# Three chained stages on one core: 128 queries an attention step from rearranged inputs, one ring for all weights, and a written order for the last stage

## The chip, the core and the metric

The kernel runs on one core of a Trainium2 chip. A core has five engines with an instruction queue each: TensorE (PE; its weight loads are listed apart as PEld), VectorE (DVE), ScalarE (ACT), GpSimd (POOL) and SyncE (SP, which here only issues DMAs). Data is brought from HBM by 16 DMA engines into SBUF, a memory of 128 partitions; TensorE writes its products into PSUM, eight banks of 2 KB a partition. The metric is the device time of one execution in microseconds (us), taken as the median of several runs.

## The reference

Everything is chained: the attention's output is the input of the mixture of experts, whose output is the input of the last network.

```python
# 1 attention: B,H,S,D = 2,8,768,64; a query sees keys nearer than 16 and 24 block summaries
k_sum = k.reshape(B, H, 24, 32, D).max(axis=3)
v_sum = v.reshape(B, H, 24, 32, D).mean(axis=3)
scores_l = where(abs(pos_q - pos_k) < 16, scale * q @ k.T, -1e9)
scores_s = scale * q @ k_sum.T + log(32)
a = softmax(concat([scores_l, scores_s]))      # sum + 1e-9 below
x = a @ concat([v, v_sum])                     # -> 1536 tokens x 512
# 2 experts: E = 8, w1[e] 512x1024, w2[e] 1024x512
do = x @ w_skip > 0
e = argmax(x[do] @ w_gate);  gate = softmax(x[do] @ w_gate)[e]
x[do] += gate * relu(x[do] @ w1[e]) @ w2[e]
# 3 last network: w_in 512x2048, w_out 2048x512, alpha 2048 (w_in and w_out in float64)
h = x @ w_in
out = (max(h, 0) + alpha * min(h, 0)) @ w_out
```

## The kernel before

**Attention.** A step takes 64 queries of all 8 heads; there are 24 steps. q and k arrive as they lie in memory, and TensorE transposes them (lines 187, 240 and 268). The transposed queries are put into a tile `qbd` in which the two heads of a pair stand on the diagonal with zeros beside them, so that one matmul with 128 rows and 128 columns gives both heads. A step is: a matmul that writes the mask (`s<-mask,sel`, L284), four score matmuls (L286), the maximum on DVE (`nm`, L289), four exponentials on ACT that also sum (`p`, L293), a product with the reciprocal sum on POOL (L305), four transposes (`pt`, L311) and their copy (`ts`, L315), eight matmuls with the values (`xp`, L327; a query sees a window of 96 keys and 24 summaries, so 120 rows). After each 128 tokens the result is transposed (`xtp`, L420), multiplied with the gate weights (`lt`, L432) and folded into the routing logits (`lg`, L442). The block means of v come for the first batch from a matmul with an averaging matrix (`vps`, L231), for the second from POOL. Everything here stands in a written order.

**Experts.** 64 tokens an expert are computed always, in pairs of experts that share one gather (`xg`); `rest` computes further tokens behind a branch where an expert has more than 64. TensorE and ACT follow the written order; DVE and POOL are ordered by a scheduler. `gpa` (L892) is the transposition of gathered tokens, `ph` (L945) the first product, `hT` (L904) the transposed hidden values, `py` (L965) the second product, `hx` (L981) the last pair's result, which `x2q` (L1108) adds to the tokens.

**Last network.** 48 units (n, j): n is one of three blocks of 512 tokens, j one of 16 slices of 128 hidden columns. A unit is 12 matmuls up (`g`, L1219) and, two units later, 12 matmuls down (`o`, L1242). Each factor is a sum of a high and a low part, and three of the four products are formed. w_in and w_out come as float64 and are turned into float32 on DVE and ACT in chunks (`f`, L641 to L649: one chunk is 128 x 512 in three steps, which the code asks for with `fill`), and split by ACT into the high part (L1182) and by POOL into the low part (`wl`, L1183). PReLU is `gs` (L1222 and L1223), its parts `ghi` (L1225, ACT) and `glo` (L1227, POOL). `prep_x2` transposes the next tokens (`x2p`, L1204) and splits them (`xl`, L1081). In this stage the scheduler orders all engines.

`F2` says after which expert how many steps of conversion are asked for. Six chunks are asked for there; the split of the first weights stands in the last network's loop:

```python
F2 = (0, 0, 3, 3, 3, 3, 3, 3)
    if c == 0 and n == 0:
        split_in(j)
        fill(FJ)          # FJ = 5
        split_out(j)
    up(n, j)
    if c == 0 and j == 1 and n + 1 < NBL:
        prep_x2(n + 1)
```

Of the kernel before, what the change touches and what calls it, by code (L numbers as in the profile page):

```python
# [22 lines left out]

def bf16_parts(x, n):
    out = []
    for _ in range(n):
        b = (np.float32(x).view(np.uint32) + np.uint32(0x8000)) & np.uint32(0xFFFF0000)
        h = float(b.view(np.float32))
        out.append(h)
        x = x - h  # L30
    return out


@with_exitstack
def tile_kernel(ctx: ExitStack, tc: tile.TileContext, q, k, v, w_skip, w_gate, w1, w2, w_in, w_out, alpha, out):
    nc = tc.nc
    B, H, S, D = q.shape
    NP = H // 2
    NS = S // 64
    NB = S // 32  # L40
    NC = S // 256
    NK = 120
    LT = 3
    LX = 4
    NV = 4
    RB = 4
# [11 lines left out]
    HE = E // 2  # L58

    const = ctx.enter_context(tc.tile_pool(name="const", bufs=1))  # L60
    ring = ctx.enter_context(tc.tile_pool(name="ring", bufs=8))
# [13 lines left out]
    qbd = []  # L75
    for i in range(2):
        qbd.append(apool.tile([128, 4, NP, 2, 64], F32, name=f"qbd{i}"))

    def clear(t, eng):
        eng.memset(t[0:64, :, :, 1, :], 0.0)  # L80
        eng.memset(t[64:128, :, :, 0, :], 0.0)

    clear(qbd[0], nc.vector)


    sel = apool.tile([67, 128], BF16, name="sel")
    nc.gpsimd.memset(sel, 1.0)
    nc.gpsimd.memset(sel[0:64, :], 0.0)
    nc.gpsimd.affine_select(
        out=sel[0:64, :].rearrange("p (h x) -> p h x", h=2), in_=sel[0:64, :].rearrange("p (h x) -> p h x", h=2),  # L90
        pattern=[[0, 2], [-1, 64]], compare_op=ALU.not_equal, fill=1.0, base=0, channel_multiplier=1,
    )
    mask = apool.tile([67, 3, NK], BF16, name="mask")
    nc.gpsimd.memset(mask, 0.0)
    logs = bf16_parts(math.log(32.0), 3)
    mlog = mask[64:67, :, 96:NK]
    nc.gpsimd.memset(mlog, logs[0])
    for i in (1, 2):
# [26 lines left out]
    def win(s):
        return (0, 0) if s == 0 else ((2, 32) if s == NS - 1 else (1, 16))

    vt = [apool.tile([NK, NV, H * D], F32, name=f"vt{b}") for b in range(B)]
    xs = {}

    kst, qst, kw, vbk, st = {}, {}, {}, {}, {}
    late, after = [], []
    V, A, P = nc.vector.tensor_copy, nc.scalar.copy, nc.gpsimd.tensor_copy
    ka, kb, km, spare = {}, {}, {}, []

    def load(src, b, c, tag):
        pool, rt_, n = (kpool, "raw", RB) if tag != "qst" else (apool, "qraw", 1)
        raw = pool.tile([128, H, 2, D], F32, tag=rt_, bufs=n, name=f"raw{tag}{b}_{c}")
        nc.sync.dma_start(raw, src[b, :, 256 * c:256 * c + 256, :].rearrange("h (p r) d -> p h (r d)", r=2))
        st[tag, b, c] = raw  # L140

    def stage(b, c, tag, bufs, eng):
        t = (kpool if tag == "kst" else apool).tile([128, 2, H, D], F32, tag=tag, bufs=bufs, name=f"{tag}{b}_{c}")
        eng(t.rearrange("p r h d -> p h r d"), st.pop((tag, b, c)))
        (kst if tag == "kst" else qst)[b, c] = t

    vbd = dram.tile([B, H, NB, D], F32, name="vbd")

    def load_vblk(b, i):
        src = v[b, 4 * i:4 * i + 4].rearrange("h (n t) d -> (h n) (t d)", t=32)  # L150
        for u in range(2):
            t = kpool.tile([96, 16, D], F32, tag="raw", bufs=RB, name=f"vbk{b}_{i}_{u}")
            nc.sync.dma_start(t, src[:, 16 * D * u:16 * D * u + 16 * D])
            vbk[b, i, u] = t

    def mean_v(b, i, step):
        t, t1 = vbk[b, i, 0], vbk[b, i, 1]
        if step < 2:
            w = slice(8 * step, 8 * step + 8)
            nc.gpsimd.tensor_tensor(out=t[:, w, :], in0=t[:, w, :], in1=t1[:, w, :], op=ALU.add)  # L160
        elif step == 2:
            nc.gpsimd.tensor_tensor(out=t[:, 0:8, :], in0=t[:, 0:8, :], in1=t[:, 8:16, :], op=ALU.add)
        else:
            for w in (4, 2, 1):
                nc.gpsimd.tensor_tensor(out=t[:, 0:w, :], in0=t[:, 0:w, :], in1=t[:, w:2 * w, :], op=ALU.add)
            m = kpool.tile([96, D], F32, tag="vm", bufs=2, name=f"vm{b}_{i}")
            nc.gpsimd.tensor_scalar(out=m, in0=t[:, 0, :], scalar1=1.0 / 32.0, scalar2=None, op0=ALU.mult)
            st["vm", b, i] = m

    def put_v(b):  # L170
        for i in range(2):
            nc.sync.dma_start(vbd[b, 4 * i:4 * i + 4].rearrange("h n d -> (h n) d"), st["vm", b, i])
        for j in range(NV):
            nc.sync.dma_start(
                vt[b][96:NK, j, :].rearrange("n (h d) -> n h d", h=H), vbd[b].rearrange("h n d -> n h d"))

    def load_vwin(b, s):
        k0 = 64 * s - win(s)[1]
        nc.sync.dma_start(
            vt[b][0:96, s % NV, :].rearrange("p (h d) -> p h d", h=H),  # L180
            v[b, :, k0:k0 + 96, :].rearrange("h p d -> p h d"),
        )

    def first_k(c):
        def part(ps, n, dst, src):
            x = kst[0, src][:, r, 2 * g:2 * g + 2, :].rearrange("p h d -> p (h d)")
            nc.tensor.transpose(ps[:, r, dst:dst + n], x[128 - n:128], ident[128 - n:128, 128 - n:128])

        if c == 0:
            for g in range(NP):  # L190
                (pool, tag) = ((ps_s, "s"), (ps_s, "s"), (ps_t, "t"), (ps_t, "t"))[g]
                ka[g] = pool.tile([128, 2, 256], F32, tag=tag, name=f"ka{g}")
                kw[0, g] = kpool.tile([128, NS, NK], F32, tag="kw", bufs=NP, name=f"kw0_{g}")
                km[g] = apool.tile([128, NB], F32, tag="ks", bufs=4, name=f"ks0_{g}")
        if c == 1:
            for g in range(NP):
                (pool, tag) = ((ps_m, "m"), (ps_m, "m"), (ps_m, "m"), (ps_x, "x"))[g]
                full = pool.tile([128, 512], F32, tag=tag, name=f"kb{g}")
                kb[g] = full[:, 0:384].rearrange("p (r i) -> p r i", r=2)
                spare.append(full[:, 384:512])  # L200
        for g in range(NP):
            for r in range(2):
                part(*((ka[g], 128, 128 * c, c) if c < 2 else (kb[g], 128, 64, 2)))
        if c == 1:
            for g in range(NP):
                for r in range(2):
                    part(kb[g], 64, 0, 1)

    def first_max(half, g, eng=nc.vector):
        ps, o = (kb[g][:, :, 64:192], 16) if half else (ka[g], 0)  # L210
        n = ps.shape[2] // 16
        eng.tensor_reduce(
            out=km[g][:, o:o + n], in_=ps.rearrange("p r (n i) -> p n r i", n=n), axis=AX.XY, op=ALU.max)
# [1090 lines left out]
```

## Time and profile before

| what | us |
|---|---|
| runs | 544.91 to 545.46, median 545.08 |
| the profiled execution | 544.38 |
| its span, first to last instruction | 542.6 |
| PE, DVE, ACT, POOL busy in the span | 498.7, 313.4, 164.9, 193.9 |

The profiled execution is 1.8 us longer than the span, and 0.7 us below the median of the runs. A busy time is a sum over the whole span and says nothing about a stage; the rows below are therefore by stage. The granted clock is full speed where it reads 1.00. Each float32 matmul leaves two records in the trace, so that "x8" in a row is four matmuls.

### The profile page before, as it was taken

Reading aid. Unit: us, or ns where it says so; the run is one execution under the profiler, and the core shown is the slowest. Engines: PE = TensorE matmul, PEld = TensorE weight load, DVE = VectorE, ACT = ScalarE, POOL = GpSimd, SP = SyncE. Lnnn points to the kernel's source line nnn. Section 1 sums busy time; section 2 is a strip of 40 time slices with the busy share of each in tenths; the row PEclk is TensorE's granted clock in tenths of the full one; section 3 lists DMA queues with packets and bytes.
Section 4 is the critical chain, followed back from the end, with each engine's and each line's share of the span. In section 5 each row is a group of like instructions: output and inputs, shape, how many; then the busy total and the mean of one; then the engine's idle time right before and its main releaser. Section 6 shows DMA issues by size and latency. Waiting matters only on the chain.

```text
span 542.6 us, 8283 instructions
## 1 busy us (share of the span) xinstructions
PE 498.7 (92%) x2999; PEld 372.7 (69%) x2999; DVE 313.4 (58%) x632; ACT 164.9 (30%) x452; POOL 193.9 (36%) x196
## 2 busy tenths in 40 slices
PE   7988999978899999596499899999999999999997
PEld 5577888853454454265277788888888888888885
DVE  4579666476431854289999739893624324243333
ACT  3666677730011110333444442531120101101010
POOL 5285523336220310324853244733453221212121
PEclk9989999998999999898879999999999999999999
DMA  9899979863999583484445402210000000001022
GB/s 240 229 257 247 278 208 277 240 212 109 383 390 396 183 296 118 150 267 143 136 156 170 142 0 79 77 39 1 0 1 0 2 0 2 0 1 59 20 77 77
DMA packets 66820, 76.81 MB, mean 142 GB/s; under 512 B 23358, under 2 KB 46930, under 8 KB 66764
## 3 DMA queue, kind: packets, MB, share of 16 engines
q1 hardware_dynamic: 55916, 59.67, 35.4%
q10 hardware_dynamic: 9408, 14.68, 8.5%
q0 software_dynamic: 1440, 1.76, 1.0%
q8 instruction: 29, 0.48, 0.4%
q14 instruction: 27, 0.22, 0.1%
HBM read 71.00 MB, written 7.91 MB: 145 GB/s over the span
## 4 chain that ended last, share of the span: by engine, by line
PE 49%; DVE 4%; POOL 2%; issue 1%; DMA 1%; ACT 1%; ACTq 0%; POOLq 0%; DVEq 0%
PE o L1242 24%; PE g L1219 24%; POOL wl L1183 1%; DMA raw<-in_moe_w_in_dram 1%; PE ph L945 1%; DVE f L643 1%; DVE f L649 1%; DVE f L648 1%; DVE xl L1081 1%; DVE acc L1252 1%; PE x2p L1204 0%; DVE f L641 0%; POOL glo L1227 0%; ACT raw L644 0%; ACT acc L1250 0%
## 5 line engine op out<-in xcount | busy, mean ns | idle before, releaser
L1227 POOL TENSOR_TENSOR glo<-gs,ghi 128x512 fp32r<-128x512 f32 x48 | 66.7, 1390 | 157.1 <-ACT ghi L1225 157.1
L1222 DVE TENSOR_SCALAR gs<-g,al 128x512 f32<-128x512 f32 x48 | 35.9, 749 | 109.7 <-PE g L1219 109.7
L1225 ACT CAST ghi<-gs 128x512 fp32r<-128x512 f32 x48 | 29.9, 622 | 176.4 <-PE o L1242 150.9
L1242 PE MATMUL o<-woh,ghi 128*128 128x512 f32 x192 | 76.3, 397 | 5.3 <-ACT ghi L1225 5.3
L1242 PE MATMUL o<-woh,glo 128*128 128x512 f32 x192 | 76.4, 398 | 3.0 <-POOL glo L1227 3.0
L1242 PE MATMUL o<-wl,ghi 128*128 128x512 f32 x192 | 76.4, 398 | 0.0
L1219 PE MATMUL g<-xh,wih 128*128 128x512 f32 (+1 forms) x196 | 53.6, 395 | 2.7 <-DVE xl L1081 1.4
L1219 PE MATMUL g<-xl,wih 128*128 128x512 f32 (+1 forms) x196 | 53.0, 390 | 1.1 <-DVE xl L1081 1.1
L1219 PE MATMUL g<-xh,wl 128*128 128x512 f32 (+1 forms) x196 | 51.5, 385 | 0.0
L1242 PEld LDWEIGHTS o<-woh,ghi 128*128 128x128 f32 x192 | 36.4, 190 | 13.7 <-ACT ghi L1225 5.5
L1219 PEld LDWEIGHTS g<-xh,wih 128*128 128x128 f32 x196 | 36.8, 190 | 11.4 <-issue 1.7
L1242 PEld LDWEIGHTS o<-woh,glo 128*128 128x128 f32 x192 | 36.3, 189 | 11.9 <-POOL glo L1227 3.8
L1219 PEld LDWEIGHTS g<-xl,wih 128*128 128x128 f32 x196 | 36.6, 188 | 9.5 <-DVE xl L1081 1.5
L1242 PEld LDWEIGHTS o<-wl,ghi 128*128 128x128 f32 x192 | 36.5, 190 | 8.2
L1219 PEld LDWEIGHTS g<-xh,wl 128*128 128x128 f32 x196 | 36.4, 188 | 7.8
L945 PE MATMUL ph<-w,gTa 128*64 128x512 f32 x128 | 32.9, 626 | 9.4 <-PEq L1148 5.5
L305 POOL TENSOR_TENSOR p<-p,sm 128x480 f32<-128x480 f32 x23 | 24.1, 1049 | 47.2 <-DVE sm L304 21.5
L293 ACT ACTIVATE p<-s,nm 128x120 f32<-128x120 f32 x96 | 33.5, 365 | 22.7 <-DVE sm L303 19.7
L644 ACT ACTIVATE raw<-raw 128x512 f32<-128x512 f32 x32 | 21.7, 684 | 42.6 <-DVE f L643 41.0
L1223 DVE SCALAR_TENSOR_TENSOR gs<-g,gs 128x512 f32<-128x512 f32 x48 | 33.0, 687 | 1.0
L1183 POOL TENSOR_TENSOR wl<-f,wih 128x512 fp32r<-128x512 f32 x16 | 23.3, 1462 | 20.7 <-ACT wih L1182 18.7
L648 DVE SCALAR_TENSOR_TENSOR f<-raw,f 128x512 int32<-128x512 int32 x32 | 30.4, 954 | 0.3
(213 smaller groups left out, 816.4 us busy)
## 6 DMA issues: line engine op xcount, KB each, us to landing
w<-in_moe_w_dram SPq DMA_DIRECT2D x30, 1024.0 KB
raw<-in_moe_w_in_dram ACTq DMA_DIRECT2D x14, 512.0 KB
raw<-in_moe_w_out_dram ACTq DMA_DIRECT2D x14, 512.0 KB
vt<-in_v_dram SPq DMA_DIRECT2D x24, 192.0 KB
rawqst<-in_q_dram SPq DMA_DIRECT2D x6, 512.0 KB
rawkst<-in_k_dram SPq DMA_DIRECT2D x6, 512.0 KB
xd<-x SPq DMA_DIRECT2D x12, 256.0 KB
out_dram<-acc SPq DMA_DIRECT2D x12, 256.0 KB
```

Of the source, the lines that this page charges most:

```text
L293: nc.scalar.activation(p[:, g, :], sp[:, g, :], AF.Exp, bias=nm[:, g:g + 1], scale=1.0, accum_out=sm[:, g:g + 1])
L305: eng.tensor_tensor(out=p, in0=p, in1=sm.to_broadcast([128, NP, NK]), op=ALU.mult)
L644: nc.scalar.activation(raw.bitcast(F32)[:, :, 0], raw.bitcast(F32)[:, :, 1], AF.Abs)
L648: nc.vector.scalar_tensor_tensor(out=f, in0=m1, scalar=-0x40000000, in1=f, op0=ALU.bitwise_and, op1=ALU.bitwise_or)
L945: nc.tensor.matmul(hp[e][64 * h:64 * h + 64, :], gT[g][:, kc, o:o + 64], a[kc // 2][:, kc % 2, 512 * h:512 * h + 512], start=(kc == 0), st ...
L1183: nc.gpsimd.tensor_tensor(out=lo, in0=f, in1=hi.bitcast(F32), op=ALU.subtract)
L1219: nc.tensor.matmul(ph[:, o], a[:, kc, :], x[kc // 2][:, kc % 2, o], start=(i == 0), stop=(i == 3 * KC - 1))
L1222: nc.vector.tensor_scalar(out=g, in0=ph, scalar1=0.0, scalar2=al[:, j:j + 1], op0=ALU.min, op1=ALU.mult)
L1223: nc.vector.scalar_tensor_tensor(out=g, in0=ph, scalar=0.0, in1=g, op0=ALU.max, op1=ALU.add)
L1225: nc.scalar.copy(ghi, g)
L1227: nc.gpsimd.tensor_tensor(out=glo, in0=g, in1=ghi.bitcast(F32), op=ALU.subtract)
L1242: nc.tensor.matmul(po[i], a[:, o], x, start=(jj == 0 and p == 0), stop=(jj == JC - 1 and p == 2))
```

## The change

The host hands over q and k already transposed, v as windows with a column of ones behind each head, the gate and skip weights side by side and alpha as columns. A step of attention takes 128 queries, so there are 12. Scores are formed in 64 x 64 quarters of the array: r is the head of a pair (which rows of the array), c the half of the queries (which columns). The sum of a softmax comes out of the ones column, and the division is done on the 128 x 512 result by DVE (`sub_n`) instead of on the probabilities by POOL. All big tiles, from raw k to the split weights and the output's accumulators, share one ring of 17 places. In the expert stage DVE stands in a written order too; conversions begin one expert earlier (FC) and come to eight chunks; eight splits (EARLY) stand behind experts 5, 6 and 7. The last network is in a written order on all engines; its next tokens are prepared one or two tiles a unit.

```diff
-    ring = ctx.enter_context(tc.tile_pool(name="ring", bufs=8))
+    NRING = 17
+    ring = ctx.enter_context(tc.tile_pool(name="ring", bufs=NRING))
...
-    ps_m = att.enter_context(tc.tile_pool(name="ps_m", bufs=3, space=PSUM))
+    ps_m = att.enter_context(tc.tile_pool(name="ps_m", bufs=1, space=PSUM))
...
-        nc.tensor.matmul(sp, sel, mask[:, win(s)[0], None, :].to_broadcast([67, NP, NK]), start=True, stop=False)
-        for g in range(NP):
-            nc.tensor.matmul(
-                sp[:, g, :], d[:, s % 4, g].rearrange("p h x -> p (h x)"), kw[b, g][:, s, :], start=False, stop=(g == NP - 1))
...
+        for g in range(NP):
+            for c in range(2):
+                for r in range(2):
+                    o = 128 * (t % 2) + 64 * c
+                    nc.tensor.matmul(
+                        sp[r][64 * c:64 * c + 64, g, :], qs[64 * r:64 * r + 64, g, o:o + 64],
+                        kw[b, g][64 * r:64 * r + 64, 2 * t + c, :], start=False, stop=(g == NP - 1))
...
-            nc.scalar.activation(p[:, g, :], sp[:, g, :], AF.Exp, bias=nm[:, g:g + 1], scale=1.0, accum_out=sm[:, g:g + 1])
+            nc.scalar.activation(
+                p[:, g, :], st["s", n][r][:, g, :], AF.Exp, bias=st["nm", n][:, r, g:g + 1], scale=SCALE)
...
+        nc.vector.reciprocal(out=sm, in_=sm)
+        xs[n] = t = apool.tile([128, H * D], F32, tag="x", bufs=3, name=f"x{n}")
+        nc.vector.tensor_tensor(
+            out=t.rearrange("p (k h d) -> p k h d", k=2, h=4), in0=x[:, :, :, 0:D],
+            in1=sm.to_broadcast([128, 2, 4, D]), op=ALU.mult)
...
-    F2 = (0, 0, 3, 3, 3, 3, 3, 3)
+    FC = (0, 3, 3, 4, 4, 4, 4, 2)
...
-    me.enter_context(tc.manual_schedule(engines={mybir.EngineType.PE, mybir.EngineType.Activation}))
+    EARLY = {5: ((0, 0), (1, 0), (0, 1)), 6: ((1, 1), (0, 2), (1, 2)), 7: ((0, 3), (1, 3))}
+    me.enter_context(tc.manual_schedule(engines={mybir.EngineType.PE, mybir.EngineType.Activation, mybir.EngineType.DVE}))
...
+        for o, j in EARLY.get(n, ()):
+            (split_in, split_out)[o](j)
...
+    if MANUAL:
+        fe.enter_context(tc.manual_schedule())
+    for i, (n, j) in enumerate(work):
+        c, k = i // per, i % per
+        up(n, j)
+        if c == 0:
+            for t in {1: (4, 5), 2: (6, 7), 3: (8,), 4: (9,), 5: (10,), 6: (11,)}.get(k, ()):
+                prep_x2(t // NB2, t % NB2)
```

On PE, in the middle of the attention, one step of 64 queries before stands in these rows (`kw` are the key windows of a pair of heads, `qbd` the queries, `p` the probabilities):

```order
L284 LDWEIGHTS sel
L284 MATMUL s_11_1542<-mask,sel 128x480
L286 MATMUL s_11_1542<-kw_0_520,qbd_87 128x120
L286 MATMUL s_11_1542<-kw_1_585,qbd_87 128x120
L286 MATMUL s_11_1542<-kw_2_646,qbd_87 128x120
L286 MATMUL s_11_1542<-kw_3_766,qbd_87 128x120
L311 MATMUL pt_8_1559<-ident,p_8_1401 120x128 x4
L327 MATMUL xp_6_1518<-vt_132,ts_7_1538 64x64 x8
L432 MATMUL lt_1573<-xT_1540,wg 32x128 x4
```

One step of 128 queries of the changed kernel, of whose 16 score matmuls four and of whose eight groups of value matmuls two stand here (`s_0` and `s_1` are the banks of the two heads of a pair):

```order
L315 MATMUL lg_643<-fold,lts_600 128x9
...
L178 MATMUL s_0_646<-mask,sel 64x480
...
L178 MATMUL s_1_647<-mask,sel 64x480
...
L185 MATMUL s_0_646<-kw_0_128,q_2_161 64x120
L185 MATMUL s_1_647<-kw_0_128,q_2_161 64x120
...
L301 MATMUL xtp_668<-ident,x_627 128x128 x4
L207 MATMUL pt_0_684<-ident,p_0_576 120x128 x4
L207 MATMUL pt_1_691<-ident,p_1_602 120x128 x4
L309 MATMUL lt_698<-xT_673,wg 32x128 x4
L218 MATMUL xp_710<-vt_106,ts_0_586 64x65 x2
L218 MATMUL xp_710<-vt_106,ts_1_593 64x65 x2
```

A score matmul now fills 64 rows of its bank, and there are 16 where two steps before had eight; the logits of an earlier tile (`lg`) now open the step ahead of the scores, and `xtp` and `lt` of the next tile follow in the same step.

On DVE, at the passage from the experts to the last network, before (`f` are chunks under conversion, `hx` the last expert's result, `xl` the low parts of the tokens):

```order
L641 TENSOR_SCALAR f_5_4102<-raw_5_3969 128x512
L981 TENSOR_SCALAR hx_1972<-py_3864,lgate 64x256 x2
L649 SCALAR_TENSOR_TENSOR f_4_4020<-raw_4_3961,f_4_4020 128x512
L643 SCALAR_TENSOR_TENSOR f_5_4102<-raw_5_3969,f_5_4102 128x512
L641 TENSOR_SCALAR f_5_4152<-raw_5_4016 128x512
L1081 TENSOR_TENSOR xl_0_3894<-x2q_3827,xh_0_3892 128x2x128
L648 SCALAR_TENSOR_TENSOR f_5_4102<-raw_5_3969,f_5_4102 128x512
L1081 TENSOR_TENSOR xl_1_3895<-x2q_3827,xh_1_3893 128x2x128
L1081 TENSOR_TENSOR xl_0_3894<-x2q_3832,xh_0_3892 128x2x128
L649 SCALAR_TENSOR_TENSOR f_5_4102<-raw_5_3969,f_5_4102 128x512
```

The same passage of the changed kernel (`gs` is PReLU of the first units):

```order
L494 SCALAR_TENSOR_TENSOR f_3_3632<-raw_3_2954,f_3_3632 128x512
L774 TENSOR_SCALAR hx_1776<-py_3698,lgate 64x256 x2
L900 TENSOR_TENSOR xl_3723<-x2q_3657,xh_3722 128x2x128
L900 TENSOR_TENSOR xl_3723<-x2q_3662,xh_3722 128x2x128
...
L1014 TENSOR_SCALAR gs_0_3801<-g_0_3776,al 128x512
L1015 SCALAR_TENSOR_TENSOR gs_0_3801<-g_0_3776,gs_0_3801 128x512
L1014 TENSOR_SCALAR gs_1_3821<-g_1_3808,al 128x512
L1015 SCALAR_TENSOR_TENSOR gs_1_3821<-g_1_3808,gs_1_3821 128x512
L900 TENSOR_TENSOR xl_3829<-x2p_3832,xh_3828 128x2x128 x2
```

Between `hx` and the second `gs` no conversion is left on DVE; the conversions of j = 0 to 3 stand ahead of `hx`.

## Rows read from the trace of the kernel before

**Rows 1.** Stretches: us, busy PE, PEld, DVE, ACT, POOL, PEclk, DMA share, GB/s.
```profile
0.00:127.50 127.50, 114.34 (x1124) 92.26 (x1124) 84.28 (x272) 75.38 (x286) 56.30 (x95) 0.96 0.88 240
127.50:244.20 116.70, 104.85 (x648) 53.06 (x648) 56.97 (x113) 18.50 (x33) 27.69 (x25) 0.99 0.73 259
244.20:300.40 56.20, 41.37 (x197) 33.80 (x197) 54.30 (x82) 23.78 (x51) 29.94 (x19) 0.88 0.47 152
...
150.00:160.00 10.00, 9.69 (x78) 5.09 (x76) 4.14 (x10) 1.16 (x3) 2.87 (x3) 1.00 1.04 392
```
**Rows 2.** Chain of waits in the last network: start, us, engine, line.
```profile
306.13 2.76 PE g L1219 x12
311.66 2.76 PE g L1219 x12
...
530.22 6.27 PE o L1242 x27
```
**Rows 3.** Timeline of PE in the attention: start, us, line, form, records.
```profile
99.80 1.05 PE L286 MATMUL s<-kw,qbd 128*128 128x120 f32 x8
...
103.00 0.37 PE L284 MATMUL s<-mask,sel 67*128 67x480 bf16 x1
103.21 1.05 PE L286 MATMUL s<-kw,qbd 128*128 128x120 f32 x8
104.09 0.60 PE L311 MATMUL pt<-ident,p 128*120 128x128 f32 x4
104.62 1.15 PE L327 MATMUL xp<-vt,ts 120*64 120x64 f32 x16
105.70 0.42 PE L432 MATMUL lt<-xT,wg 128*32 128x128 f32 x8
106.55 0.66 PE L420 MATMUL xtp<-ident,x 128*128 128x128 f32 x4
107.22 0.39 PE L442 MATMUL lg<-fold,lts 128*128 128x9 f32 x2
```
**Rows 4.** The same view: block means of v.
```profile
17.79 5.33 PE L231 MATMUL vps<-rawvst,avg 128*24 128x512 f32 x12
```
**Rows 5.** Groups by line: busy, mean ns; idle before, releaser.
```profile
L289 DVE TENSOR_REDUCE nm<-s 128x4 f32<-128x480 f32 x24 | 15.7, 656 | 25.2 <-PE s L286 25.1
L293 ACT ACTIVATE p<-s,nm 128x120 f32<-128x120 f32 x96 | 33.5, 365 | 22.7 <-DVE sm L303 19.7
L293 ACT ACTIVATION_READ_ACCUMULATOR p<-s,nm 128x1 f32 x96 | 20.0, 208 | 0.0
L315 ACT COPY ts<-pt 120x512 f32<-120x512 f32 x24 | 14.2, 595 | 0.9 <-PE xp L327 0.9
...
L648 DVE SCALAR_TENSOR_TENSOR f<-raw,f 128x512 int32<-128x512 int32 x32 | 30.4, 954 | 0.3
...
L1222 DVE TENSOR_SCALAR gs<-g,al 128x512 f32<-128x512 f32 x48 | 35.9, 749 | 109.7 <-PE g L1219 109.7
```
**Rows 6.** Timeline of PE and DVE from the experts' start; waits in brackets.
```profile
127.50 0.66 PE L892 MATMUL gpa<-ident,xg 128*128 128x128 f32 x4 [0.80 <-DMA xg<-xd,lidx]
...
144.89 1.93 PE L945 MATMUL ph<-w,gTa 128*64 128x512 f32 x7 [1.47 <-issue]
...
226.57 3.26 PE L945 MATMUL ph<-w,gTa 128*64 128x512 f32 x8 [5.46 <-PEq L1148]
...
240.51 3.67 PE L965 MATMUL py<-w,hT 128*64 128x256 f32 x32 [0.56 <-DVE hT L904]
246.75 5.26 PE L1108 MATMUL x2q<-oc,hx 128*128 128x128 f32 x32 [2.57 <-DVE hx L981]
...
250.33 2.04 DVE L648 SCALAR_TENSOR_TENSOR f<-raw,f 128x512 int32<-128x512 int32 x1
...
267.03 0.80 PE L1242 MATMUL o<-woh,ghi 128*128 128x512 f32 x1 [5.26 <-ACT ghi L1225]
...
271.71 0.79 PE L1242 MATMUL o<-woh,glo 128*128 128x512 f32 x1 [3.04 <-POOL glo L1227]
```

More of the change, by code (lines that the diff above doesn't have):

```diff
@@ L21, with tile_kernel @@
 DRAM = bass.MemoryType.DRAM
[L24 to L31, printed above, removed]
 @with_exitstack
-def tile_kernel(ctx: ExitStack, tc: tile.TileContext, q, k, v, w_skip, w_gate, w1, w2, w_in, w_out, alpha, out):
+def tile_kernel(ctx: ExitStack, tc: tile.TileContext, qt, kt, vwin, vtok, vblk, wgs, als, w1, w2, w_in, w_out, out):
     nc = tc.nc
[L37 to L46, printed above, removed]
+    B, NCH, _, NP, QW = qt.shape
+    SP = kt.shape[3]
+    NTB, NWK, NV, H, DV = vwin.shape[1:]
+    D = DV - 1
+    S = NTB * 128
+    NB, NS = S // 32, S // 64
+    NK = NWK + NB
     SCALE = 1.0 / math.sqrt(D)
@@ L72, in tile_kernel @@
+    V, A, P = nc.vector.tensor_copy, nc.scalar.copy, nc.gpsimd.tensor_copy
+    xs, st, kw, qc, vt, vbk = {}, {}, {}, {}, [], {}
     ident = const.tile([128, 128], F32, name="ident")
     make_identity(nc, ident)
[L75 to L86, printed above, removed]
@@ L125, in win @@
[L125 to L140, printed above, removed]
@@ L142, in stage @@
[L142 to L154, printed above, removed]
@@ L201, in first_k @@
         for g in range(NP):
[L202 to L205, printed above, removed]
+            for c in range(2):
                 for r in range(2):
[L207 to L213, printed above, removed]
@@ new lines, in sub_t, with sub_x @@
+        copy(ts, pt)
+        st["ts", n, r] = ts
+    def sub_x(n):
+        b, t = divmod(n, NTB)
+        ts = [st.pop(("ts", n, r)) for r in range(2)]
+        st["x", n] = xp = ps_x.tile([128, 2, 512], F32, tag="x", name=f"xp{n}")
+        for h in range(H):
+            for c in range(2):
+                nc.tensor.matmul(
+                    xp[64 * c:64 * c + 64, h // 4, DV * (h % 4):DV * (h % 4) + DV],
+                    ts[h % 2][:, h // 2, 64 * c:64 * c + 64], vt[b][:, 2 * (t % 2) + c, h, :], start=True, stop=True)
@@ L678, in tile_kernel, with warm @@
+    def warm(n):
+        t = ps_t.tile([128, 512], F32, tag="t", name="warm")
+        for i in range(n):
+            nc.tensor.matmul(t, rt["ones"], rt["rows"].bitcast(BF16)[:, 0:512], start=True, stop=True)
     ms = ExitStack()
     ms.enter_context(tc.manual_schedule())
-    load(q, 0, 0, "qst")
-    for c in range(NC):
-        load(k, 0, c, "kst")
-    hot(HOT[0])
-    stage(0, 0, "qst", 1, V)
-    stage(0, 0, "kst", 3, V)
-    first_k(0)
-    prep_q(0, 0, 0, A)
-    prep_q(0, 0, 1)
-    for c in range(NC):
-        load(v, 0, c, "vst")
@@ L819, in tile_kernel @@
-    route_a(*G[2])
-    for t in range(4 + NPL, 8):
-        route_c(t)
-    sub_x(*subs[NN - 2])
-    tile_xt(TT - 2)
-    flush(late)
-    sub_x(*subs[NN - 1], copy=both)
-    tile_lt(TT - 2)
-    flush(late)
-    for f in todo[NN + 1]:
-        f()
-    tile_xt(TT - 1)
-    route_b(*G[2])
-    tile_lg(TT - 2)
-    flush(late)
-    tile_lt(TT - 1)
-    route_l(*G[2], [8])
-    flush(after)
-    flush(late)
-    tile_lg(TT - 1)
-    flush(after)
-    route_a(*G[3], between=lambda: route_c(9))
+        if n >= 2:
+            put_x(n - 2)
@@ new lines, in tile_kernel @@
+    n = TT - 1
+    tile_lg(n - 3)
+    rt["small"] = ps_s, "s"
+    tile_xt(n - 2)
+    sub_t(n, 0, V)
+    sub_t(n, 1, A)
+    tile_lt(n - 2)
+    sub_x(n - 1)
+    sub_n(n - 1)
+    tile_lg(n - 2)
+    put_x(n - 1)
+    for f in todo[TT]:
+        f()
+    sub_x(n)
+    route_a(*G[2])
+    tile_xt(n - 1)
+    sub_n(n)
+    put_x(n)
+    for f in todo[TT + 1]:
+        f()
+    warm(2)
+    route_b(*G[2])
+    tile_lt(n - 1)
+    tile_xt(n)
+    tile_lg(n - 1)
+    route_l(*G[2], [])
+    warm(2)
@@ L1291 @@
     arrays, args = {}, []
-    for name in _INS:
-        a = np.ascontiguousarray(inputs[name])
+    for name, a in layouts(inputs).items():
+        a = np.ascontiguousarray(a)
         if a.dtype == np.float64:
```

714 lines of the change are left out of this document (283 added, 431 removed).

## Prediction

> **What bounds the kernel now.** I cut the span by stage first, because the shares of the whole span mix three limits [rows 1]. From 0 to 127.5 us is the attention with its routing: PE is busy 114.3 of 127.5 us, at a granted clock of 0.96, so its own instruction list is nearly the bound. From 127.5 to 244.2 us are the experts: PE is busy 104.9 of 116.7 us and waits 11.9 us. From 244.2 to 300.4 us the last network starts, with PE busy for only 41.4 of 56.2 us; DVE is busy for 54.3 there. Then the chain of waits consists of PE alone [rows 2]: a unit begins every 5.53 us (306.13 to 311.66, twice 2.76 us of matmuls), and the last matmul ends at 536.5, 6.1 us ahead of the span's end at 542.6. For the time after 300.4 us nothing in the change takes a matmul away. So three terms can move: the attention (A), the experts (B) and everything behind the last expert matmul (C). The profiled execution is 544.4 us: 127.5 + 116.7 + 298.4 + 1.8 around the span; it stands 0.7 us under the median of the runs, which I leave in the range.
>
> **A, attention.** The PE work of one step, from single row groups [rows 3]: before, for 128 queries, twice (mask 0.37, scores 1.05, pt 0.60, xp 1.15) and once xtp 0.66, lt 0.42, lg 0.39: 7.81 us. The step is measured at 103.21 - 99.80 = 3.41 us for 64 queries, 6.82 for 128. Row groups thus overlap: 6.82/7.81 = 0.87. The transposes of q and k come on top of this and go entirely, with the copies into qbd.
>
> After the change a step holds four masks, 16 score matmuls, 8 transposes, 16 value matmuls and the same routing. No row of before has a matmul of 64 rows and 64 columns, so the price is bounded. A score matmul costs 1.05/4 = 0.26 us. If each runs alone, 16 cost 4.2 us and the masks 4 x 0.37 = 1.5; if two run side by side, 2.1 and 0.74; if four, 1.05 and 0.37. The nearest row is py [rows 6]: 16 matmuls of 256 columns that alternate between the column halves, in 3.67 us, 0.23 each. A score matmul of 120 columns takes 0.26 by itself, so these clearly run in pairs. I take two side by side. The value matmuls are in pairs of halves too: 1.6 us, between 1.15 and 2.3. Sum: 2.1 + 0.74 + 1.2 + 1.6 + 0.66 + 0.42 + 0.39 = 7.1, times 0.87 = 6.2 us a step.
>
> The other bound is the loop through the engines. `lg` of a tile opens the step and needs `lts`, which ACT copies behind the step's first four exponentials, and they need the maximum. So: lg and scores about 2.2, two maxima of 0.66 [rows 5] and the scaling 1.4, four exponentials 0.85 to 1.46 (0.365 each when alone), a copy of `ts` 0.6, `lts` 0.3: 5.3 to 6.1 us. ACT's sum per 128 queries is 8 x 0.365 + 1.5 = 4.4 us, since the 208 ns of reading the accumulator, 96 times, go. DVE gets the division on 512 columns, an estimate of 0.9 us by gs's 0.75 for as many and two small operations [rows 5], beside 1.4 and 0.6: hidden. I take 6.1 us a step.
>
> The start: 2.2 MB must land (q 0.5, k 1.6); at the 240 GB/s of the stretch [rows 1] this is 9 us, then a reduction, a copy and the scores: first scores end at about 13. Eleven steps at 6.1 are 67. The vps matmul of 5.33 us [rows 4] stands in step 1, in which PE otherwise lacks xp and the routing: net +1.9. The reductions of the second batch's k on DVE and the routing of the first four tiles stand ahead of the next maximum: +4. Last scores end at 13 + 67 + 1.9 + 4 = 86. From there to the first expert transpose it was 104.3 + 23.2 = 127.5 before (the last pt, xp and three routings in a row). After, three tiles instead of four queues of 64 are left, with the division in the chain: 26. So A = 112, a gain of 15.5. The new layouts of v, wg and alpha belong to this term; I cost them at nothing, since the same data was loaded before.
>
> A rule speaks against this. The Trainium skill, "TensorEngine Tiling (Array Packing)", "Tiling Modes", "Key Properties", says that the tiles work independently of each other, but that a change of the tiling mode drains the engine. The kernel changes shape about five times a step. No row of before shows such a drain apart: the overlap of 0.87 was measured across row groups with three shapes in each step. By its first sentence four would run at once, which is the first rival; by its second a step would be longer, which belongs to the last.
>
> **B, experts.** PE's instruction list is the same. The wait of 1.47 us at 144.89 for weights [rows 6] should go, since 13 pieces instead of 12 are loaded ahead. The 5.46 us at 226.57 are at a branch (PE's sequencer) and stay. DVE does 57 us in the stretch [rows 1]; two more chunks add four operations each, the third of 0.95 us on the mean [rows 5], so at most 3.8 us a chunk; I take 3.3, and DVE comes to 64 of 115 us: covered, with at most 6.6 us uncovered if they stand ahead of hT, for which the second product waits. Eight splits go to ACT (18.5 us busy of 116.7) and POOL (27.7 busy): nothing, at most the place of one ahead of an activation. B = 115.2, bounds 112 to 122.
>
> **C, the last network.** Its 298.4 us run from the last expert matmul, 240.51 + 3.67 = 244.2 [rows 6]. In the first 56.2 us PE lacks 14.8. Of this 2.57 are the wait for hx, 5.26 the first down matmul's wait for ghi and 3.04 that for glo, all with DVE at conversions (2.04 us for one at 250.33). With four slices converted and split before, only xl and the two operations of gs (0.75 each [rows 5]) stand ahead of ghi, and ghi and glo then lie beside the second and third up of 2.76 us each. I leave 3 of the 14.8 us: C = 286.6, bounds 283.6 (none left) and 298.4 (all). The 24 other chunks come at most one a unit: 3.3 + 1.5 of gs = 4.8 of 5.53 us on DVE, hidden behind PE by 0.7 us. This cover is the thinnest; at 3.8 us a chunk and with xl beside it, it is gone in the units that prepare tokens too, about 0.5 us in each of three.
>
> **Sum.** 112 + 115.2 + 286.6 + 1.8 = 515.6; I say 515.
>
> **Rivals.**
> Four at once: scores 1.05 and masks 0.37, so PE falls to 5.0 us a step and the loop, with shorter scores, to about 5.1. A = 112 - 11 x 0.95 = 101.5, total 505. For: the four matmuls of a pair of heads use four different quarters in turn. Against: in py only two can go together, so no row shows four.
> The start of the last network stays as it is: the written order puts prep_x2 of two tiles a unit between the first gs, so that the stall moves from conversion to xl and to the loads of the tokens. C = 298, total 527. For: eight xl and four loads of tokens stand in the units 1 and 2. Against: they come behind gs of the same unit.
> Transfers: about 32 MB by the first gather (inputs 14, x written 3, weights 14) need 286 GB/s; the same stretch had 240, an expert stretch 392 [rows 1]. At 260 it is 123 us, but only the last weight pieces, which the third expert wants, are late: +8, total 523.
> The quarters run one by one: the slower case. Scores 4.2, masks 1.5, xp 2.3, so 10.6 x 0.87 = 9.3 us a step; A = 112 + 11 x 3.2 = 147, total 550. It decides against the kernel from A = 112 + 29 = 141, a step of 6.1 + 29/11 = 8.7 us. Where score matmuls alone run one by one, it is (7.1 + 2.1) x 0.87 = 8.0 us and 536: not slower. For: rows of the array have not been seen to work side by side. Against: py. A drain at each of five shapes would add to it.
>
> **How the numbers follow.** Forecast 0.47; four at once 0.19; start of the last network unchanged 0.13; transfers 0.08; one by one 0.13, half of it on the slower side. The forecast's own range is 508 to 523. Over all it is 496 to 535: it takes in four at once with a shorter end and both cases at 523 to 527, and leaves out the case of one by one and the tail of the first rival. A change under 0.2% (1.1 us) cannot be told from none. Faster by more 0.92, within 0.02, slower 0.06.
>
> **What will show it.** Right: masks begin every 6.1 us in the middle of the attention; the first gpa at about 112; between the last py and the first unit only x2q and its hx wait of about 1 us; the first down matmul without a wait over 1 us; units at 5.53 us. Wrong: a pitch under 5.4 or over 8 (A); `ph` waiting for DMA in the first three experts (B); PE waiting for gs, ghi or xl between the first six units, or units over 5.6 us while conversions run (C).

## The result and the profile after

The changed kernel takes 522.59 us (median of four runs, 517.99 to 524.53) against 545.0 us: a ratio of 0.958, with an interval of 0.953 to 0.963. The profiled execution is the shortest of the four, 517.99 us with a span of 516.3; its stages are therefore compared with the forecast's terms, and the 4.6 us to the median are taken up further below.

The stretches of the changed kernel, cut at the same events as [rows 1] (columns as there: us, busy PE, PEld, DVE, ACT, POOL, granted clock, DMA share, GB/s):

```profile
0.00:111.04 111.04, 83.13 (x1243) 59.64 (x1243) 67.29 (x219) 48.38 (x151) 30.56 (x70) 0.91 0.91 286
111.04:228.98 117.94, 105.26 (x648) 53.24 (x648) 58.59 (x115) 18.39 (x34) 33.25 (x27) 0.97 0.68 243
228.98:285.18 56.20, 52.56 (x267) 44.44 (x268) 34.31 (x61) 18.48 (x42) 16.47 (x13) 0.97 0.21 68
285.18:510.05 224.87, 219.22 (x955) 179.76 (x954) 142.16 (x196) 51.67 (x85) 79.16 (x61) 0.99 0.16 52
```

| term | before | forecast | measured |
|---|---|---|---|
| A, to the first expert transpose | 127.5 | 112 | 111.0 |
| B, experts | 116.7 | 115.2 | 117.9 |
| C, from the last expert matmul to the span's end | 298.4 | 286.6 | 287.3 |

PE's work in the attention fell from 114.3 to 83.1 us, but the stage only by 16.5: PE now waits 27.9 us there, where it waited 13.2. The start of the last network lost most of its wait, as forecast (3.6 us idle in 56.2, before 14.8). What was not forecast is a wait for the accumulators' copies: 3.1 of these 3.6 us, and with it most of the 5.6 us of idle PE in the last row, a stretch in which PE had never waited before.

A late step of the attention, PE's timeline of the changed kernel, to be read beside [rows 3] (start, us, line, form, records):

```profile
78.79 0.40 PE L178 MATMUL s<-mask,sel 64*64 64x480 bf16 x4
79.02 0.99 PE L185 MATMUL s<-kw,q 64*64 64x120 f32 x32
79.94 0.66 PE L301 MATMUL xtp<-ident,x 128*128 128x128 f32 x4
80.43 1.04 PE L207 MATMUL pt<-ident,p 128*120 128x128 f32 x8
81.40 0.43 PE L309 MATMUL lt<-xT,wg 128*32 128x128 f32 x8
81.75 1.15 PE L218 MATMUL xp<-vt,ts 120*64 120x65 f32 x32
83.46 0.39 PE L315 MATMUL lg<-fold,lts 128*128 128x9 f32 x2 [0.56 <-ACT lts L311]
83.78 0.40 PE L178 MATMUL s<-mask,sel 64*64 64x480 bf16 x4
84.01 0.99 PE L185 MATMUL s<-kw,q 64*64 64x120 f32 x32
```

The 16 score matmuls take 0.99 us, where eight took 2.10 in two steps before; the four masks take about as long as one (0.40 and 0.37). The step is 83.78 - 78.79 = 5.0 us. The last scores end at 85.0 and the expert transpose begins at 111.04.

The chain of waits in the last network, beside [rows 2]:

```profile
307.43 2.72 PE g L1011 x12
310.15 2.72 PE o L1034 x12
312.87 2.72 PE g L1011 x12
315.59 2.51 PE o L1034 x11
...
503.92 6.13 PE o L1034 x27
```

A unit takes 5.44 us instead of 5.53, and the chain is broken after 315.59. What PE waited for in this stage (engine and line waited for: us, times, longest):

```profile
PE o L1034 <- ACT acc L1042: 7.4, 3, 3.5
PE o L1034 <- ACT wih L868: 0.8, 2, 0.4
PE x2q L927 <- DVE hx L774: 0.6, 1, 0.6
PE o L1034 <- ACT woh L868: 0.4, 1, 0.4
```

The 8.3 us of the first down matmuls' waits for ghi and glo [rows 6] are gone, and the wait for hx fell from 2.57 to 0.58. In their place stands a wait for `acc`, the copies that free the banks of one block of tokens for the next. The two waits of the first 56 us, in PE's timeline:

```profile
229.56 3.84 PE L927 MATMUL x2q<-oc,hx 128*128 128x128 f32 x32 [0.58 <-DVE hx L774]
...
270.28 0.80 PE L1034 MATMUL o<-woh,ghi 128*128 128x512 f32 x1 [3.06 <-ACT acc L1042]
```

### The profile page after: what moved, and what is told of

The parts are those of the page before. It is cut to its first block, busy times and chain, and to the rows that moved or that the text cites. A ratio compares the mean times of both kernels' runs of the same rounds, so it can differ in the third digit from the quotient of the medians.

```text
span 516.3 us, 8189 instructions
## 1 busy us (share of the span) xinstructions
PE 462.2 (90%) x3118; PEld 338.4 (66%) x3118; DVE 305.1 (59%) x594; ACT 136.9 (27%) x311; POOL 159.4 (31%) x170
## 4 chain that ended last, share of the span: by engine, by line
PE 49%; DVE 6%; ACT 2%; issue 1%; ACTq 0%; DVEq 0%
PE o L1034 24%; PE g L1011 21%; PE py L758 1%; DVE f L494 1%; DVE f L488 1%; PE ph L738 1%; PE x2q L927 1%; PE x2q L920 1%; DVE f L493 1%; DVE f L486 1%; PE x2p L996 1%; DVE gs L1014 1%; DVE gs L1015 1%; DVE acc L1044 1%; ACT raw L489 1%
## 5 line engine op out<-in xcount | busy, mean ns | idle before, releaser
L1019 POOL TENSOR_TENSOR glo<-gs,ghi 128x512 fp32r<-128x512 f32 x48 | 62.4, 1299 | 139.1 <-ACT ghi L1017 139.1
L1034 PE MATMUL o<-wol,ghi 128*128 128x512 f32 x192 | 76.0, 396 | 0.0
L1011 PE MATMUL g<-xh,wih 128*128 128x512 f32 (+1 forms) x196 | 51.7, 386 | 0.0
L1011 PE MATMUL g<-xh,wil 128*128 128x512 f32 (+1 forms) x196 | 51.5, 385 | 0.0
L1034 PEld LDWEIGHTS o<-wol,ghi 128*128 128x128 f32 x192 | 36.8, 192 | 7.4
L1011 PEld LDWEIGHTS g<-xh,wil 128*128 128x128 f32 x196 | 36.4, 188 | 7.3
L494 DVE SCALAR_TENSOR_TENSOR f<-raw,f 128x512 f32<-128x512 f32 x32 | 32.2, 1008 | 10.1 <-ACT raw L489 8.5
L199 ACT ACTIVATE p<-s,nm 128x120 f32<-128x120 f32 x96 | 27.1, 385 | 10.5 <-DVE nm L194 7.6
L758 PE MATMUL py<-w,hT 128*64 128x256 f32 x256 | 29.2, 381 | 0.0
L869 POOL TENSOR_TENSOR wil<-f,wih 128x512 fp32r<-128x512 f32 x16 | 20.7, 1291 | 27.4 <-ACT wih L868 24.4
```

The source lines that it names most:

```text
L199: nc.scalar.activation(p[:, g, :], st["s", n][r][:, g, :], AF.Exp, bias=st["nm", n][:, r, g:g + 1], scale=SCALE)
L494: nc.vector.scalar_tensor_tensor(out=t, in0=raw.bitcast(F32)[:, :, 0], scalar=TINY, in1=t, op0=ALU.is_ge, op1=ALU.mult)
L758: nc.tensor.matmul(py[64 * d:64 * d + 64, 0:256], lhs, w2_rows(e, fc)[:, 256 * d:256 * d + 256], start=(fc == 0), stop=(fc == 7))
L869: nc.gpsimd.tensor_tensor(out=lo, in0=f, in1=hi.bitcast(F32), op=ALU.subtract)
L1011: nc.tensor.matmul(ph[:, o], a[:, kc, :], x[kc // 2][:, kc % 2, o], start=(i == 0), stop=(i == 3 * KC - 1))
L1019: nc.gpsimd.tensor_tensor(out=glo, in0=g, in1=ghi.bitcast(F32), op=ALU.subtract)
```

## Experiments

**How the quarters of the array share the work.** Three kernels have the same 16 score matmuls in another order of the loops over g (pair of heads), c (column half) and r (row half); the masks and the value matmuls keep theirs. Nested loops are written on one line here.

```diff
-        for g in range(NP): / for c in range(2): / for r in range(2):
+        for c in range(2): / for r in range(2): / for g in range(NP):     # q_serial
+        for r in range(2): / for g in range(NP): / for c in range(2):     # q_cols
+        for c in range(2): / for g in range(NP): / for r in range(2):     # q_rows
```

> The 16 score matmuls of a step in another order: the four of one quarter of the array one behind the other, then the next quarter. In the changed kernel the 16 take 0.99 us, 0.06 each, where one of 120 columns cost 0.26 before. Theory (four quarters work at once, and the order is what lets them): the four of one quarter cannot overlap, so the group takes about 3.5 us (16 x 0.22), a step gets longer by some 2.5 us, the attention by up to 27, and the whole comes to 535 to 545 us. Rival (small matmuls of 64 rows are cheap in themselves): the group stays at 1.0 us and the time at 518 to 524.

> The same 16 score matmuls, but neighbours in the queue alternate only between the two column halves (halves of the queries); the row half (the head of a pair) changes once in a step. Theory: two at once, group about 2.0 us, whole about 528 us. If column halves did not overlap: 3.5 us, as with one quarter behind the other. If only the count of rows mattered: 1.0 us.

> The same 16 score matmuls, but neighbours alternate only between the two row halves (the heads of a pair); the column half changes once in a step. Theory: row halves overlap as column halves do, group about 2.0 us, whole about 528 us. Rival that the forecast held (only column halves work side by side): 3.5 us and 535 to 545 us.

One score group from PE's timeline of q_serial, in a step at full clock:

```profile
91.44 2.38 PE L185 MATMUL s<-kw,q 64*64 64x120 f32 x32
```

The same of q_cols:

```profile
93.72 1.46 PE L185 MATMUL s<-kw,q 64*64 64x120 f32 x32
```

And of q_rows:

```profile
86.27 1.46 PE L185 MATMUL s<-kw,q 64*64 64x120 f32 x32
```

One quarter behind the other 2.38 us, two side by side 1.46, four 0.99. Row halves work side by side as column halves do, and the order in the queue decides it. But even one by one a matmul costs 2.38/16 = 0.15 us, not the 0.26 taken from [rows 3], where a matmul filled 128 rows. All three groups came out shorter than I expected of them. The one execution of each took 535.01, 531.3 and 524.23 us. q_cols and q_rows have the same group time and differ by 7 us, so these runs rank the groups and not the totals.

**The early splits.** late_split takes the splits and two of the eight chunks out of the expert stage.

```diff
-    EARLY = {5: ((0, 0), (1, 0), (0, 1)), 6: ((1, 1), (0, 2), (1, 2)), 7: ((0, 3), (1, 3))}
-    FC = (0, 3, 3, 4, 4, 4, 4, 2)
+    EARLY = {}
+    FC = (0, 3, 3, 3, 3, 3, 3, 0)
+        if c == 0 and n == 0:
+            split_in(j)
+            split_out(j)
         up(n, j)
```

> The early splits are taken out of the expert stage: six chunks are converted there as before, and the splits of the first four slices stand in the first four units of the last network, ahead of the unit's up matmuls, with the two chunks that are missing converted there. The written order of all engines stays. Theory (the early split is what took the start-up wait away): the waits of the first units come back, 8 to 12 us, about 530 us. Rival (the written order of DVE did it, since conversions no longer slip between the first PReLUs): at most 2 us more than the changed kernel.

It takes 538.31 us (ratio to before 0.984, 0.980 to 0.988). From its PE timeline:

```profile
244.43 2.07 PE L1011 MATMUL g<-xh,wih 128*128 128x512 f32 x4 [2.74 <-ACT wih L868]
...
254.06 1.73 PE L1011 MATMUL g<-xh,wih 128*128 128x512 f32 x4 [4.23 <-ACT wih L868]
...
268.86 2.07 PE L1011 MATMUL g<-xh,wih 128*128 128x512 f32 x4 [6.55 <-ACT wih L868]
```

The waits come back, 13.5 us where 8 to 12 were expected, and after each the group of four records takes 1.7 to 2.1 us instead of 1.07, at a granted clock of 0.85 in the first 56 us of the stage. C is 307.6 us in this trace, 9 us more than before. But the profiled execution, 543.41 us, is the longest of the six; if its 5 us above the median all lie in C, it is about 4 us more (an estimate). Without the early splits this written order is worse than the scheduler was.

**The written order of the last network.** sched_last has MANUAL = False and keeps the early splits.

> Only the order of the last network is given back to the scheduler; the early splits stay. Theory (early splits took the start-up wait away; the written order added the waits for acc of 7.4 us, since ACT's copy stands behind a split): the start stays without waits over 1 us, the waits for acc go, and units return to the 5.53 us of before if the scheduler was what set that; 48 x 0.09 = 4.3 us more, so within 4 us of the changed kernel either way, 515 to 524. Rival (the written order is needed at the start as well): conversions slip ahead of the first PReLUs again and it is 530 us or more.

533.12 us (0.981, 0.973 to 0.989). The wait did not go, it grew. PE's waits in its last stage:

```profile
PE o L1034 <- ACT acc L1042: 6.4, 1, 6.4
PE g L1011 <- DVE xl L900: 1.8, 2, 1.1
PE x2q L927 <- DVE hx L774: 1.7, 1, 1.7
```

This is its first 66 us; over the whole stage the waits for acc come to 11.6. On ACT the scheduler too put other work in front of the copies: splits of weights, a conversion and the tokens' `xh`, which waits 3.89 us for DVE. C is 296.2. So in the traces early splits alone give 2 us of C's 11, the written order alone minus 9 (at the median perhaps minus 4), and both together 11. Units stay at 5.44 us: the scheduler is not what made them 5.53. My theory was wrong in both points.

**DVE's written order in the experts.** sched_dve takes DVE from the list of engines in written order.

> Only DVE in the expert stage is given back to the scheduler. In the changed kernel the stage takes 117.9 us where 115.2 was forecast; DVE waits there 2.32 us for the first float64 chunk, with the next expert's list behind it, and PE waits 2.09 us for that. Theory (the written order put the conversion ahead of the list): the wait goes, the stage is 2 us shorter; but conversions may then stand ahead of hx, 1 to 3 us more at its end. About 520 us. Rival (the wait is one for the weights or for the list itself): it stays, and the stage takes 118 us or more.

526.95 us (0.968, 0.962 to 0.973). PE's waits in its expert stage, those that the changed kernel does not have or has elsewhere:

```profile
PE py L758 <- DVE hT L697: 3.9, 1, 3.9
PE phb L808 <- DVE xt_more L688: 3.3, 1, 3.3
...
PE lb L789 <- issue: 2.0, 1, 2.0
```

The stage takes 127.2 us. The wait of 2 us for which I had blamed the order of DVE stays, so that theory falls, and conversions get ahead of hT as the forecast's bound for B had it. In the traces the written order is worth 9 us in this stage; by the medians the whole kernel is 4.4 us slower without it (526.95 against 522.59), since the changed kernel's trace is of its shortest execution.

**Copies ahead of the split.** down_first moves one call.

```diff
-        if c + 1 < NG:
-            ... split of the next weights ...
         if i >= LD:
             down(*work[i - LD])
+        if c + 1 < NG:
+            ... split of the next weights ...
```

> In the last network the split of the next weights is written behind the unit's down matmuls and their accumulator copies instead of ahead of them. Theory: the three waits for acc (3.1, 3.5 and 0.8 us) come from ACT and DVE, which have a conversion and a split to do first; moved behind, the waits go, and with them the half clock that follows the first (about 2 us): 8 to 10 us less, 510 to 515. Rival (the copies themselves are too slow for the one group of up matmuls, 2.7 us, that covers them): at most 3 us less.

509.66 us (0.936, 0.931 to 0.941). Its first 56 us of the last network and the rest:

```profile
231.36:287.56 56.20, 55.62 (x289) 47.27 (x289) 37.15 (x64) 19.66 (x43) 18.64 (x15) 1.00 0.24 76
287.56:501.40 213.84, 211.89 (x934) 174.85 (x933) 142.18 (x193) 51.36 (x83) 76.84 (x60) 1.00 0.16 52
```

PE is idle for 0.6 and 2.0 us, where it was 3.6 and 5.6, and at full clock it is busy for 267.5 us instead of 271.8 for the same work: 6.7 us of waits and 4.3 us of half clock behind them make the 11 us by which C falls. For the most part the copies are not too slow; they stood behind a split that itself waited for a conversion. The 2.0 us that are left are two waits for acc.

**Three more moves.** v_all and, part by part, down_vt and nm_act; all three hold down_first's move as well.

```diff
-            (A, V, A, V)[j](vt[0][96:NK, j, :, 0:D], src)          # v_all, down_vt, nm_act
+            A(vt[0][96:NK, j, :, 0:D], src)
-    n = (3, 3, 4, 5)[g]                                            # v_all, nm_act
+    n = (2, 3, 4, 5)[g]
-    FC = (0, 3, 3, 4, 4, 4, 4, 2)                                  # v_all
+    FC = (0, 0, 4, 4, 4, 4, 4, 4)
-        nc.vector.tensor_scalar(out=nm, in0=nm, scalar1=-SCALE, scalar2=None, op0=ALU.mult)   # nm_act
+        nc.scalar.mul(nm, nm, -SCALE)
```

> down_first, and three more moves: conversions begin one expert later (0, 0, 4, 4, 4, 4, 4, 4), the block means are copied by ACT alone so that the second step's maximum does not stand behind two of the copies on DVE, and the four reductions of the second batch's k stand in steps 2, 3, 4 and 5 instead of two in step 3. Theory: 2.3 us (wait for the first chunk) + 1.6 + 2.0 on top of down_first, about 505 us. Rival (the attention's steps hide the one, the branch the other): no more than 1 us below down_first.

515.39 us (0.943, 0.936 to 0.950), 6 us above down_first and 10 above the theory; one of its four executions took 510.29. Its expert transpose begins at 115.5, and the wait of 2.2 us in the experts is there again. DVE's timeline in its step 4:

```profile
37.59 1.22 DVE L193 TENSOR_REDUCE nm<-s 128x4 f32<-128x480 f32 x2 [1.37 <-PE s L185]
38.85 4.49 DVE L194 TENSOR_SCALAR nm<-nm 128x8 f32<-128x8 f32 x1
```

POOL's in the same stretch:

```profile
38.83 2.49 POOL L153 TENSOR_TENSOR vbk<-vbk 96x512 f32<-96x512 f32 x2
41.27 0.81 POOL L117 COPY kw<-kraw 128x768 f32<-128x768 f32 x1
42.05 1.25 POOL L155 TENSOR_TENSOR vbk<-vbk 96x512 f32<-96x512 f32 x1
```

An operation on eight columns stands on DVE for 4.49 us, from POOL's start to POOL's pause; in the eleven other steps of this trace it takes 0.17. Reductions from PSUM are not held: in the changed kernel two that begin at 28.33, with POOL's additions running from 28.30 on, take 1.22 us as elsewhere, and the scaling right behind them takes 1.25. What PE then waits for in v_all's step, and in the same step of nm_act below:

```profile
45.24 0.39 PE L315 MATMUL lg<-fold,lts 128*128 128x9 f32 x2 [3.90 <-ACT lts L311]
```

```profile
40.27 0.39 PE L315 MATMUL lg<-fold,lts 128*128 128x9 f32 x2 [0.54 <-ACT lts L311]
```

> down_first with only one of the three other moves of v_all: the block means are copied by ACT alone. In v_all the third step's masks came 2.7 us sooner after the second's than in the changed kernel; theory: that part was good, and what spoiled v_all is the reductions moved to step 2 (the waits for lts of 2.5 and 3.9 us) and not this: 507 to 509 us. Rival (the executions differ by that much in the clock alone): 509 to 512, as down_first.

509.63 us (0.932, 0.929 to 0.935): the rival. Its median is down_first's, although in its trace two of its steps (masks from 25.93 to 35.16) take 2.2 us less than down_first's (25.37 to 36.75). The trace is of its longest execution, whose expert transpose begins at 113.9 against 111.8, behind a wait of 1.49 us for q and the half clock shown below. Whether its shorter executions keep the 2.2 us is not shown.

> down_vt with the reductions of the second batch's k in steps 2, 3, 4 and 5 as in v_all, and the scaling of the maxima (128 x 8) done by ACT instead of DVE. In v_all that operation of eight columns stood on DVE from 38.85 to 43.34 us, which is just while POOL worked without a pause (38.83 to 43.30), and PE waited 3.9 us for what follows. Theory (DVE cannot do that operation, from SBUF to SBUF, beside POOL's): on ACT it takes 0.2 us, the wait goes, and the attention is 4 us shorter than v_all's, the whole 504 to 508. Rival (DVE waited for a semaphore, or POOL slows ACT in the same way): the step stays near 10 us.

507.66 us (0.931, 0.926 to 0.937). ACT scales in 0.21 us, and the step that took 9.95 us in v_all (masks at 35.61 and 45.56) takes 4.97 (35.62 and 40.59). Of these 5.0 us 3.4 are the wait above; the rest is PE at a lower clock in v_all's step (its 16 scores there take 1.64 us, in nm_act 0.99). The expert transpose begins at 110.6, 4.9 us ahead of v_all's. The theory is shown for that step; as a whole it is the fastest kernel here by its median, but its interval overlaps those of down_first and down_vt.

> The changed kernel once more, unchanged, so that the runs of the other two stand beside it on one chip, and for a second trace of it: its first profiled execution was 4 us shorter than the other three. Theory: the difference is in stretches at half the clock, which begin at the same waits of PE (routing on DVE, the branch, the accumulator copies) and last longer: the same instruction list, mean clock 0.960 instead of 0.967. Rival: another wait for data.

523.59 us (519.55 to 527.46; 0.961, 0.955 to 0.968). The profile again fell on the shortest execution, with the same waits and the same clock of 0.967, so that a long execution of this kernel was not seen in a trace. One of a relative was: down_vt's profiled execution is its longest (513.11 of 508.35 to 513.11), and its stretch from 65 us on shows it (columns as in the first fence):

```profile
65.00:85.00 20.00, 16.64 (x252) 13.83 (x250) 9.83 (x27) 9.49 (x31) 0.00 (x0) 0.77 0.77 242
```

The same stretch of down_first:

```profile
65.00:85.00 20.00, 16.70 (x323) 14.13 (x316) 11.85 (x34) 10.00 (x33) 0.00 (x0) 0.92 0.90 287
```

As much busy time and 71 records fewer, at a mean granted clock of 0.77 instead of 0.92. The changed kernel's own executions point the same way, since each comes with its mean granted clock: 0.967 at 517.99 and 519.55 us, 0.963 at 520.70, 0.960 to 0.961 at 522.42 to 524.53, 0.954 at 526.48. A clock lower by 0.006 over 520 us costs about 3 of the 4.6 us (an estimate); in which stretches, and what the rest is, no trace shows.

## Why the prediction was right, and where only its sum was

The measured 522.6 us lie in the range (496 to 535), 7.6 above the forecast of 515. The profiled execution, 518.0, is 2.4 above the sum of 515.6: A came out 1.0 lower, B 2.7 higher, C 0.7 higher. The small differences of A and C are luck in part: both are made of larger errors that cancel. One sign that was named for A being wrong did come, a pitch under 5.4 us.

**A was right by two errors.** I took two quarters at a time, 2.1 us a group and 6.1 us a step. It is four at a time, 0.99 and 5.0 us, as the first rival had it in its own numbers. The factor 0.87 for the overlap of row groups held: the new groups sum to 5.06 us by the rows above, with 0.56 of waiting in a step of 4.99, so 4.43/5.06 = 0.88. Against this, from the end of the first scores (12.4) to that of the last (85.0) it took 72.6 us: eleven steps of 5.0 and 17.6 more, while I had 67 and 5.9. Both terms failed, by 12 us each, with opposite signs. Of the 2.05 us by which the step's groups stay under the forecast sum of 7.1, the scores are 1.1, the value matmuls 0.45 (1.15 instead of 1.6), masks and transposes the rest. Rows of PE's timeline of the changed kernel show where the 17.6 went:

```profile
19.54 6.07 PE L138 MATMUL vps<-vtok,ones 128*24 128x512 f32 x12 [0.26 <-issue]
...
37.07 0.40 PE L178 MATMUL s<-mask,sel 64*64 64x480 bf16 x4
...
40.64 0.66 PE L301 MATMUL xtp<-ident,x 128*128 128x128 f32 x4 [2.35 <-DVE lg L316]
...
43.12 2.00 PE L218 MATMUL xp<-vt,ts 120*64 120x65 f32 x32
...
45.37 0.40 PE L178 MATMUL s<-mask,sel 64*64 64x480 bf16 x4
...
57.24 0.40 PE L178 MATMUL s<-mask,sel 64*64 64x480 bf16 x4
...
64.88 0.40 PE L178 MATMUL s<-mask,sel 64*64 64x480 bf16 x4
65.11 1.47 PE L185 MATMUL s<-kw,q 64*64 64x120 f32 x32
...
73.04 0.40 PE L178 MATMUL s<-mask,sel 64*64 64x480 bf16 x4
```

From the end of one step's scores to that of the next, the step with vps takes 4.4 us more than 5.0, that behind the two reductions 3.3 (8.3 from masks to masks), and the two with the routing 3.1 and 2.7 (7.6 and 8.2 from masks to masks): 13.5 of the 17.6; the rest lies in three other steps. Part of this are waits for DVE, such as the 2.35 us above. Part is PE's own work, which does not shrink with the scores: vps takes 6.07 us, and behind such waits the clock is down (0.61 from 40.6 to 45.0 us, where xp takes 2.00 instead of 1.15, and 0.59 from 64.8 to 69.0, where the scores take 1.47). So the first rival failed as well: its 101.5 us supposed that the special steps shrink with the others. The start (first scores at 12.4, forecast 13) and the tail (26.0, forecast 26) were right. By PE's busy time per line of code in this stage (lines overlap in time, so these sums do not add up to the stage) the transposes of q and k, 16.9 us before, are gone, the scores fell from 26.5 to 15.2 us, the value matmuls from 28.0 to 14.7 and the masks from 8.9 to 6.2. The runs change only the scores' order; what the new layouts, the ones column and the ring of 17 places are worth by themselves is not shown.

**The slower case was overpriced.** I put 0.26 us on a quarter alone. q_serial shows 0.15. It serializes the score matmuls only, the case for which I had a step of 8.0 us and 536 in all; its one execution took 535.01, which agrees in the total, but with a group of 2.38 us instead of 4.2. Masks and value matmuls one by one, the rest of the slower case, were not run. The drain at a change of shape, which the Trainium skill ("TensorEngine Tiling (Array Packing)", "Tiling Modes", "Key Properties") names, has no visible price here: the row groups overlap by the same share as before with more changes in a step. The same section has the tiles work independently; the three orders agree with it.

**B missed by 2.7 us**, inside its bounds: the 1.5 us that I took off did not go. PE's timeline of the changed kernel:

```profile
131.86 0.24 PE L789 MATMUL lb<-val,ohb 128*128 128x5 bf16 x4 [2.09 <-issue]
...
211.18 3.68 PE L738 MATMUL ph<-w,gTa 128*64 128x512 f32 x8 [4.86 <-PEq L968]
```

The wait that I gave to late weights is probably not one for weights: its releaser was "issue" [rows 6], and with more pieces loaded ahead a like wait stands here. In every trace one wait of 1.5 to 2.2 us whose releaser is "issue" stands a few us behind the first branch of the experts on PE; it did not move with DVE's order, nor with the first conversion. The Trainium skill ("Runtime: NRT & Kernel Launch", "Instruction fetch mechanics") says that branching breaks the sequential prefetch of instructions, and that a taken branch whose target lies outside what has been fetched waits for it; the place agrees, and no run here shows the cause. The branch behind the sixth expert stays with 4.86 us, and the eight records behind it take 3.68 us instead of 1.94, as they took 3.26 before. The rival of late transfers did not come: the first stage moved 286 GB/s, where it supposed 260, and the one wait for weights in the experts is 0.80 us, at 172.81.

**C was right in the mechanism and by cancelling in the sum.** The waits for ghi and glo are gone and that for hx is 0.58 us, so the rival in which the start stays as it is failed. At the start 3.6 us of waiting are left, forecast 3, but 3.1 of them are the wait for acc, which I did not have. Nor did I have the 5.6 us of idle PE later. The forecast named the thin cover on DVE (0.7 us a unit on the mean) and put its end at the tokens' preparation; it broke at the accumulators, where ACT's and DVE's copies stand behind a split and a conversion. down_first shows that most of this is the order. Given back by PE's busy time, 271.8 us instead of 277.5: 48 units x 0.09 = 4.3 us are shorter matmuls, and the half clock at the start of before, x2q's 5.26 us instead of 3.84 among it, outweighs by 1.4 us the 4.3 behind the waits for acc. So 298.4 - 11.2 + 5.6 - 5.7 = 287.1. Why a matmul takes 0.227 instead of 0.230 us stays open; sched_last speaks against the order of instructions, and that it is where the tiles lie is not tested.

## What to carry to other kernels

In a written order the operation that frees a buffer belongs ahead of one that only prepares: this one move gave 13 us of 523 by the medians, 11 of them in the traced last stage. And a slack that is enough on the mean has to be checked in the unit with the most work. Here early work alone gave 2 us, a written order alone lost time, and both together gave 11, so undo each alone before crediting one. And when a step's main engine gets faster, price the steps that hold other work or hang on another engine by themselves, since they keep their length.

## What the runs showed of the hardware

Sixteen matmuls of 64 rows by 64 columns with 120 moving columns take 2.38 us on one quarter after the other, 1.46 on two at a time (column halves or row halves) and 0.99 on four, by their order in the queue alone. A small DVE operation from SBUF to SBUF stood for 4.49 us while POOL worked without a pause, 0.17 elsewhere, and reductions from PSUM were untouched; on ACT the same operation took 0.21 us beside POOL. The Trainium skill ("SBUF — State Buffer", "SBUF: two separate sides") has a port pair that POOL and some kinds of DVE operations lock against each other for a whole instruction; the trace agrees, and the hold lasted over several of POOL's instructions. Behind late_split's waits of 2.74, 4.23 and 6.55 us PE's next matmuls took 1.7 to 2.1 us for four records instead of 1.07, so that these waits cost more than their own length.
